# One list of timed steps for all five queues, single PSUM banks, and a reversing copy, in a Performer attention with an FNet block

## The chip, the cores and the metric

The kernel runs on one core of one Trainium2 chip. The core has TensorE (PE; its weight loads, which overlap, are PEld), VectorE (DVE), ScalarE (ACT), GpSimd (POOL) and SyncE (SP). Each takes its instructions in order from a queue of its own; DMAs are issued from SP, ACT or POOL and run on 16 DMA engines. The metric is the time of one execution on the device, in microseconds (us).

## The reference

All sizes: batch 8, heads 8, 576 rows, head dimension 64, 128 features; the MLP goes from 512 to 2048 and back. The MLP's weights come as float64.

```python
def phi(x):                          # for q and k, scaled
    proj = einsum('bhsd,md->bhsm', x, omega)
    h = proj - sum(x * x, -1) / 2
    return exp(h - max(h)) / sqrt(m)
kv = einsum('bhsm,bhsd->bhmd', k_p, v);  z = sum(k_p, axis=2)
attn = (q_p @ kv) / (q_p @ z + 1e-06)
x = attn with its heads side by side                 # (8, 576, 512)
u = x + real(fft(fft(x, axis=1), axis=2))
un = (u - mean(u)) / sqrt(var(u) + 1e-06)            # over the last axis
out = u + maximum(un @ w_ch1, 0) @ w_ch2
```

## The kernel before, in words

The work has four kinds of pieces, and each is written as a generator of steps (a stream).

- **Pairs** (`attn`): 32, each two heads of one batch, four per batch. k and q of the pair are loaded (`kq`, two buffers) and turned on TensorE in nine blocks (`transposed`: tps, evicted by ACT to kqT and later to qeT). Nine products with omega give 18 feature blocks (pp); DVE takes the maximum of each (nmx) and ACT the exponential (e). Nine products with v make kv (kvp, gathered in one PSUM bank), the q features are turned, and 36 matmul instructions give numerator and denominator (ndp), which DVE divides into xo. SP stores xo to DRAM (`xs`).
- **Mixing** (`mix`): one per batch, once the four pairs are stored. The Fourier transform along the rows uses symmetry: x needs rows 0 to 288 and the same rows reversed. The straight half is loaded by SP; the reversed half is gathered by three indirect DMAs from POOL with a table of row numbers (`turned`), 97 rows each. DVE folds sums, then POOL folds differences; TensorE multiplies with cosine and sine tables (yp, then ab), ACT and DVE combine, and DVE and POOL add to x. The result `us` goes to DRAM, one half by SP, the reversed half by three indirect scatters from POOL, 96 rows each.
- **Norm and MLP** (`prep`, `mlp`): 12 blocks of 384 rows. u is loaded, normalized by DVE with POOL's power, and turned (tp, unT). The first layer makes 16 tiles hp, whose Relu goes to ACT and DVE in turn, in two PSUM banks (mm); the second layer gathers 16 products in op, DVE adds u (`ur`), SP stores the output.
- **Weights** (`weights`, `narrow`): 32 tiles of 512 KB. POOL loads raw float64 words (three buffers) and clamps the high words; then ACT, DVE and POOL rebuild float32 from the bits, for which DVE runs four operations (lines 251, 255, 258, 259) and POOL the final sum (line 260).

PSUM is split into two double banks (`big`), two single ones (`sml`) and two for the MLP (`mm`).

`Listing.run` decides the order: it simulates the streams with the durations written into each `Step` and always takes the step that can start first. A `Step` has TensorE's time (`pe`), PSUM slots it holds and a chain of what follows on other engines. Only TensorE's queue keeps that order (`manual_schedule(engines={PE})`); the other four queues are ordered by the framework's own estimates. The gather is a chain entry of 9.0 us (line 425). From the 13th pair on each stream of pairs makes a pause of `PACE` = 25 us in the simulation (line 658). Of steps that can start at the same time the stream that stands first wins: norms, mixing, the two streams of pairs, weights, then the MLP (`channels`).

Of the kernel before, what the change touches and what calls it, by code (L numbers as in the profile page):

```python
# [29 lines left out]
ACT, DVE, POOL, DMA = "act", "dve", "pool", "dma"  # L30
HOP = 0.1


class Step:
# [4 lines left out]
    def __init__(self, pe=0.0, slots=(), chain=(), needed=True, when=None):  # L39
        self.pe, self.slots, self.chain = pe, slots, chain  # L40
        self.needed, self.when = needed, when


class Listing:
# [3 lines left out]
    def __init__(self, slots):  # L48
        self.free = {ACT: 0.0, DVE: 0.0, POOL: 0.0}
        self.slots = {name: [0.0] * n for name, n in slots.items()}  # L50
        self.now = 0.0

    def start(self, step, ready):
        if step.when is not None and not step.when():
            return None
        t = ready
        for name in step.slots:
            t = max(t, min(self.slots[name]))
        return t

    def run(self, streams):
        todo = [[g, next(g), 0.0] for g in streams]
        while todo:
            best = None
            for item in todo:
                t = self.start(item[1], item[2])
                if t is not None and (best is None or max(t, self.now) < best[0]):
                    best = (max(t, self.now), item)
            if best is None:
                raise RuntimeError("every stream waits")  # L70
            begin, item = best
            step = item[1]
            end = begin + step.pe
            if step.pe:
                self.now = end
            t = end
            for eng, dur in step.chain:
                t += HOP
                if eng in self.free:
                    t = self.free[eng] = max(t, self.free[eng]) + dur  # L80
                else:
                    t += dur
            for name in step.slots:
                at = self.slots[name]
                at[at.index(min(at))] = t
            item[2] = t + HOP if step.needed else end
            try:
                item[1] = next(item[0])
            except StopIteration:
                todo.remove(item)  # L90

HI_HIGH = float(np.uint32((1151 << 20) - 1).view(np.float32))
# [30 lines left out]
def kernel(  # L125
# [25 lines left out]
    CVB = 2  # L151
# [18 lines left out]
    cvt = ctx.enter_context(tc.tile_pool(name="cvt", bufs=CVB + 1))  # L170
    mlpp = ctx.enter_context(tc.tile_pool(name="mlp", bufs=2))
    dram = ctx.enter_context(tc.tile_pool(name="dram", bufs=1, space=bass.MemoryType.DRAM))
    big = ctx.enter_context(tc.tile_pool(name="big", bufs=2, space=PSUM))
    sml = ctx.enter_context(tc.tile_pool(name="sml", bufs=2, space=PSUM))
    mmp = ctx.enter_context(tc.tile_pool(name="mmp", bufs=2, space=PSUM))

    def big_tile(name):
        return big.tile([128, 2, 512], F32, name=name, tag="big")

    def sml_tile(name):  # L180
        return sml.tile([128, 512], F32, name=name, tag="sml")


    loaded = {}

    def load(n):
        b, pr = divmod(n, NP)
        h = slice(2 * pr, 2 * pr + 2)
        kq = ld.tile([P, 2 * R, D], F32, name="kq", tag="kq")
        rows = "i (p r) d -> (i p) r d"  # L190
        nc.sync.dma_start(kq[:, 0:R, :], k[b, h].rearrange(rows, r=R))
        nc.sync.dma_start(kq[:, R : 2 * R, :], q[b, h].rearrange(rows, r=R))
        loaded[n] = kq

# [7 lines left out]
    def load_v(n):  # L202
        b, pr = divmod(n, NP)
        vd = vds[n % NV]
        for i in range(2):
            nc.sync.dma_start(
                vd[D * i : D * i + D, :, (D + 1) * i : (D + 1) * i + D],
                v[b, 2 * pr + i].rearrange("(p r) d -> p r d", r=R),
            )
        loaded["v", n] = vd  # L210
# [4 lines left out]
    for n in range(NV):  # L215
        load(n)
        load_v(n)
# [4 lines left out]
    nc.gpsimd.memset(mhalf[:], -0.5)  # L222

    tabs = _tables(S, DM)
    tab_sb = {}
    for n, a in tabs.items():
        tab_sb[n] = const.tile(list(a.shape), F32, name=n + "_sb")
        src = nc.inline_tensor(a, name="k_" + n).ap()
        for p0, p1 in ((0, 96), (96, a.shape[0])):
            nc.scalar.dma_start(tab_sb[n][p0:p1], src[p0:p1])  # L230
    cs, sn, cd, sd = (tab_sb[n] for n in ("cs", "sn", "cd", "sd"))


    rows_hi = (S - CW * np.arange(NC3)[None, :] - np.arange(CP)[:, None]) % S
    turned = const.tile([CP, NC3], U32, name="turned")
    src = nc.inline_tensor(np.ascontiguousarray(rows_hi).astype(np.uint32), name="k_turned").ap()
    nc.scalar.dma_start(turned[:], src)
# [6 lines left out]
    def narrow(dst, raw):  # L244
# [18 lines left out]
    there = {"w1": 0, "w2": 0}  # L263

    def weights():
        parts = [
            (w1[:, j, f : f + CV], w1v[:, j, f : f + CV], "w1", f + CV if j == NDC - 1 else f)
            for f in range(0, DFF, CV)
            for j in range(NDC)
        ] + [(w2[:, j, :], w2v[:, j, :], "w2", j + 1) for j in range(NFC)]  # L270
        raws = []
        for i in range(len(parts) + CVB):
            if i < len(parts):
                dst, src = parts[i][:2]
                if src.dtype == F32:
                    nc.gpsimd.dma_start(dst, src)
                else:
                    raw = cvt.tile([128, CV, 2], U32, name="raw", tag="raw")
                    nc.gpsimd.dma_start(raw[:].rearrange("p n two -> p (n two)"), src.bitcast(U32))
                    raws.append(raw)  # L280
            if i >= CVB:
                dst, src, name, upto = parts[i - CVB]
                if src.dtype != F32:
                    yield Step(chain=((POOL, 0.8), (DVE, 2.8)))
                    narrow(dst, raws[i - CVB])
                there[name] = upto


    om2 = const.tile([128, 2, MF], F32, name="om2")
    nc.gpsimd.memset(om2[:], 0.0)  # L290
    omps = sml_tile("omps")
    nc.tensor.transpose(omps[:, 0:128], om[:].rearrange("m i d -> m (i d)"), ident[:])
    for i in range(2):
        rows = slice(D * i, D * i + D)
        nc.vector.tensor_scalar(om2[rows, i, :], omps[rows, 0:128], SCALE, None, op0=ALU.mult)


    xs = [dram.tile([S, DM], F32, name=f"xs{b}") for b in range(B)]
    us = [dram.tile([S, DM], F32, name=f"us{b}") for b in range(B)]

    def transposed(src, name):

        dst = att.tile([128, R, 128], F32, name=name, tag="turned")
        ps = big_tile("tps")
        p1 = sml_tile("tps1")
        for j in range(R):
            to = ps[:, j // 3, j % 3 * 128 :] if j < 6 else p1[:, (j - 6) * 128 :]
            nc.tensor.transpose(to[:, 0:128], src(j), ident[:])  # L310
        nc.scalar.activation(
            out=dst[:, 0:6, :].rearrange("q (two c) p -> q two (c p)", two=2),
            in_=ps[:, :, 0:384],
            func=AF.Copy,
        )
        nc.scalar.activation(
            out=dst[:, 6:9, :].rearrange("q c p -> q (c p)"), in_=p1[:, 0:384], func=AF.Copy
        )
        return dst

    done = {}

    def attn(n):
        b, pr = divmod(n, NP)
        yield Step(1.0, ("big", "sml"), ((ACT, 1.3),))
        kq, vd = loaded.pop(n), loaded.pop(("v", n))

        flat = kq[:].rearrange("p c d -> p (c d)")
        kqT = transposed(lambda j: flat[:, 128 * j : 128 * j + 128], "kqT")
        if n + NV < B * NP:  # L330
            load(n + NV)

# [35 lines left out]
        def feature(c):  # L368
            return es[c // 8][:, c % 8, :]
# [330 lines left out]
```

## Time and profile before

| | us |
|---|---|
| median of 3 runs (1616.69 to 1622.35) | 1617.15 |
| the profiled execution | 1618.99 |
| its span, from the first to the last instruction | 1617.2 |
| PE busy | 1449.6 (90%) |
| PEld busy | 905.3 (56%) |
| DVE busy | 456.9 (28%) |
| ACT busy | 339.3 (21%) |
| POOL busy | 324.8 (20%) |

Busy times are sums of instructions over the span. Matmuls are pipelined, so PE's busy time also holds the time in which a matmul runs at a lower clock; the granted clock (1.00 is full speed) stands beside it in the windows. Releasers of waits are inferred from semaphore events.

### The profile page before, as it was taken

The numbers are of one execution on the slowest core, as the hardware profiler recorded it, in microseconds if no ns is written. First come the engines' busy times: TensorE is split into PE (matmuls) and PEld (weight loads), VectorE is DVE, ScalarE is ACT, GpSimd is POOL, SyncE is SP. The second block draws the span as 40 slices with busy tenths as digits, with TensorE's granted clock in tenths as the row PEclk, the third lists the DMA queues.
The fourth block names the chain that finished last, engine by engine and source line by source line (L and its number), as shares of the span: only waits on it lengthen the run. The fifth ranks groups of instructions, "written<-read, shape, count | busy, mean of one in ns | idle before, by whom it ended". The sixth has DMA issues, their size and how long they took to land.

```text
span 1617.2 us, 15802 instructions
## 1 busy us (share of the span) xinstructions
PE 1449.6 (90%) x6241; PEld 905.3 (56%) x6241; DVE 456.9 (28%) x926; ACT 339.3 (21%) x925; POOL 324.8 (20%) x282
## 2 busy tenths in 40 slices
PE   5464647998999899899989989997999999999999
PEld 4453535764765576476656647555555454545453
DVE  3675763331312323132232323122110101010010
ACT  4443233231222123122212312121000000000000
POOL 5676852203102300310230031012100000000000
PEclk9776768998999999899989999998999999999999
DMA  6444433222223122222312221021110101010100
GB/s 182 139 138 110 133 121 97 63 82 65 72 59 101 47 59 70 65 72 54 102 46 65 69 66 50 15 70 32 46 38 5 53 0 59 0 59 0 40 0 26
DMA packets 132191, 103.98 MB, mean 64 GB/s; under 512 B 98596, under 2 KB 98852, under 8 KB 132118
## 3 DMA queue, kind: packets, MB, share of 16 engines
q1 hardware_dynamic: 106128, 75.63, 16.4%
q0 software_dynamic: 25344, 26.41, 5.8%
q8 instruction: 49, 0.80, 0.2%
q10 hardware_dynamic: 646, 0.94, 0.2%
q14 instruction: 24, 0.20, 0.0%
HBM read 74.50 MB, written 28.31 MB: 64 GB/s over the span
## 4 chain that ended last, share of the span: by engine, by line
PE 71%; DMA 12%; POOL 9%; DVE 4%; issue 3%; ACT 1%; SPq 0%; POOLq 0%; DVEq 0%; ACTq 0%
PE hp L601 30%; PE op L633 24%; DMA x<-xs,turned 7%; PE pp L345 4%; DMA raw<-in_moe_w_ch_dram 3%; PE kvp L374 3%; PE tps L310 3%; PE yp L471 3%; POOL raw L250 2%; POOL x L433 2%; PE ndp L394 2%; POOL w L260 1%; PE ab L488 1%; DMA xs<-xo 1%; DVE nmx L351 1%
## 5 line engine op out<-in xcount | busy, mean ns | idle before, releaser
L601 PE MATMUL hp<-unT,w 128*128 128x384 f32 x1536 | 514.5, 491 | 8.7 <-DVE ht L610 8.7
L633 PE MATMUL op<-w,ht 128*128 128x512 f32 x1152 | 506.8, 593 | 0.0
L601 PEld LDWEIGHTS hp<-unT,w 128*128 128x128 f32 x1536 | 291.5, 192 | 204.4 <-issue 10.7
L633 PEld LDWEIGHTS op<-w,ht 128*128 128x128 f32 x1152 | 215.4, 190 | 247.3 <-issue 243.9
L360 ACT ACTIVATE e<-pp,nmx 128x128 f32<-128x128 f32 x576 | 154.4, 405 | 182.0 <-DVE nmx L351 181.9
L345 PE MATMUL pp<-om,kqT 128*128 128x256 f32 x576 | 142.3, 399 | 18.2 <-ACT e L360 10.2
L610 DVE TENSOR_SCALAR ht<-hp 128x384 f32<-128x384 f32 x96 | 53.5, 557 | 356.8 <-PE hp L601 356.8
L612 ACT ACTIVATE ht<-hp 128x384 f32<-128x384 f32 x96 | 47.9, 499 | 492.8 <-PE hp L601 492.8
L565 POOL TENSOR_TENSOR rstd<-rstd,mhalf 128x1 f32<-128x1 f32 x36 | 20.9, 583 | 644.1 <-DVE rstd L564 635.7
L345 PEld LDWEIGHTS pp<-om,kqT 128*128 128x128 f32 x576 | 114.1, 202 | 43.7 <-ACT e L360 11.1
L351 DVE TENSOR_REDUCE nmx<-pp 128x8 f32<-128x1024 f32 (+1 forms) x96 | 89.6, 951 | 97.4 <-PE pp L345 97.0
L640 DVE TENSOR_TENSOR ur<-ur,op 128x512 f32<-128x512 f32 x36 | 24.6, 685 | 282.6 <-PE op L633 282.6
L374 PEld LDWEIGHTS kvp<-vd,e 128*128 128x128 f32 x576 | 76.9, 209 | 14.8 <-ACT e L360 7.6
L374 PE MATMUL kvp<-vd,e 128*128 128x130 f32 x576 | 78.2, 295 | 6.5 <-ACT e L360 6.5
L250 POOL TENSOR_SCALAR raw<-raw 128x512 f32<-128x512 f32 x32 | 67.7, 2117 | 49.2 <-DMA raw<-in_moe_w_ch_dram 49.0
L433 POOL DMA_INDIRECT x<-xs,turned x24 | 52.9, 2205 | 111.6 <-issue 67.5
L471 PE MATMUL yp<-cs_sb,fold 97*128 97x289 f32 x96 | 36.2, 540 | 34.5 <-DVE fold L457 31.3
L310 PE MATMUL tps<-ident,kq 128*128 128x128 f32 x288 | 43.7, 303 | 24.2 <-issue 11.2
L471 PE MATMUL yp<-sn_sb,fold 97*128 97x289 f32 x96 | 38.1, 568 | 24.4 <-ACT y L478 24.4
L310 PEld LDWEIGHTS tps<-ident,kq 128*128 128x128 f32 x288 | 37.5, 157 | 35.9 <-issue 18.3
L394 PE MATMUL ndp<-kv,qeT 128*64 128x65 f32 x1152 | 42.1, 230 | 15.4 <-DVE kv L382 14.0
L394 PEld LDWEIGHTS ndp<-kv,qeT 128*64 128x64 f32 x1152 | 37.9, 143 | 30.8 <-issue 28.7
(63 smaller groups left out, 901.2 us busy)
## 6 DMA issues: line engine op xcount, KB each, us to landing
raw<-in_moe_w_ch_dram POOLq DMA_DIRECT2D x32, 512.0 KB, 4.4
kq<-in_k_dram SPq DMA_DIRECT2D x32, 288.0 KB, 3.9
kq<-in_q_dram SPq DMA_DIRECT2D x32, 288.0 KB, 3.6
vd<-in_v_dram SPq DMA_DIRECT2D x64, 144.0 KB, 3.2
xs<-xo SPq DMA_DIRECT2D x64, 144.0 KB, 2.4
out_dram<-ur SPq DMA_DIRECT2D x36, 256.0 KB, 2.0
u<-us SPq DMA_DIRECT2D x32, 256.0 KB, 2.6
ur<-us SPq DMA_DIRECT2D x32, 256.0 KB, 2.6
```

Source lines behind the costliest of these rows:

```text
L250: nc.gpsimd.tensor_scalar(hif, hif, -HI_HIGH, HI_HIGH, op0=ALU.max, op1=ALU.min)
L310: nc.tensor.transpose(to[:, 0:128], src(j), ident[:])
L345: nc.tensor.matmul(flat_ps[:, 256 * j : 256 * j + 256], lhsT=kqT[:, 4 * t + j, :], rhs=om2[:].rearrange("p i m -> p (i m)"),)
L351: nc.vector.tensor_reduce(nmx[:], flat_ps[:, 0 : MF * num].rearrange("p (c m) -> p c m", m=MF), axis=AX.X, op=ALU.max, negate=True,)
L360: nc.scalar.activation(out=e[:, c, :], in_=flat_ps[:, MF * c : MF * c + MF], func=AF.Exp, bias=nmx[:, c : c + 1],)
L374: nc.tensor.matmul(kvp[:, 0 : 2 * (D + 1)], lhsT=feature(r), rhs=vd[:, r, :], start=(r == 0), stop=(r == R - 1),)
L394: nc.tensor.matmul(ndp[cols, r // 5, (D + 1) * (r % 5) : (D + 1) * (r % 5 + 1)], lhsT=qeT[:, r, cols], rhs=kv[:, i, :],)
L433: nc.gpsimd.indirect_dma_start(out=x[:, NC3 + c, :], out_offset=None, in_=rows[:, :], in_offset=bass.IndirectOffsetOnAxis(ap=turned[:, c : ...
L471: nc.tensor.matmul(yp[:, 0:NK], lhsT=fold[:, c, n, :], rhs=tab[:, c, :], start=(c == 0), stop=(c == NC3 - 1),)
L601: nc.tensor.matmul(hp[:], lhsT=w1[:, dc, 128 * fc : 128 * fc + 128], rhs=unT[:, dc, :], start=(dc == 0), stop=(dc == NDC - 1),)
L610: nc.vector.tensor_scalar(ht[:], hp[:], 0.0, None, op0=ALU.max)
L633: nc.tensor.matmul(yp[:], lhsT=hs[fc][:, 128 * i : 128 * i + 128], rhs=w2[:, fc, :], start=(fc == 0), stop=(fc == NFC - 1),)
```

## The change

What it does:

- A `Step` now belongs to one engine (PE, ACT, DVE, POOL, SP, or none), has a time there and a lateness after it (a DMA's landing, an eviction's end), names the events it waits for (`after`) and makes, and the buffers it takes and gives. A stream can `Fork`. `Listing` keeps all buffers and the five queues, and all five keep its order. Every DMA on SP is a step. A Relu goes to ACT or DVE, whichever ends first in the list.
- PSUM: six single banks for everything but the MLP's two. A pair's features come in groups of 4, 4, 4, 4, 2 instead of 8, 8, 2; the transposes are evicted in groups of 4, 4, 1 blocks instead of 6, 3.
- The reversed rows: after each pair's xs store, SP copies the pair's columns of rows 575 down to 288 into a second DRAM tensor `xb`; the mixing loads the reversed half from `xb` straight. The gather goes; the scatter of `us` stays.
- `narrow` has no clamp: high words beyond float32's range are no longer limited. ACT reads the raw high words and writes the scaled value to the destination first; DVE's four operations and POOL's sum follow.
- Tables are loaded by SP after the second pair's inputs instead of by ACT at the start; the weights start after the second pair's q has landed.

```diff
+    def __init__(self, eng, us=0.0, late=0.0, after=(), makes=None, take=(), give=()):
...
+    def start(self, step, ready, before):
+        t = ready[0] if before in step.engines and len(step.engines) == 1 else ready[1]
+        for ev in step.after:
+            if ev not in self.made:
+                return None
+            t = max(t, self.made[ev])
...
+        eng = min(step.engines, key=lambda e: max(t, self.free[e]) + step.engines[e])
+        return max(t, self.free[eng] if eng != NONE else 0.0), eng
...
+            end = begin + step.engines[eng]
+            self.free[eng] = end
+            done = end + step.late + (HOP if eng != NONE else 0.0)
...
+            item[3], item[4] = (end, done), eng
...
+    psum = ctx.enter_context(tc.tile_pool(name="psum", bufs=6, space=PSUM))
...
-        nc.gpsimd.tensor_scalar(hif, hif, -HI_HIGH, HI_HIGH, op0=ALU.max, op1=ALU.min)
-        nc.vector.tensor_scalar(bits, hi, 0x80000000, None, op0=ALU.bitwise_and)
-        nc.scalar.activation(out=hif, in_=hif, func=AF.Copy, scale=2.0**-112)
+        yield Step(ACT, 0.7, after=(("raw", i),))
+        nc.scalar.activation(out=dst, in_=hif, func=AF.Copy, scale=2.0**-112)
+        yield Step(DVE, 0.6)
+        nc.vector.tensor_scalar(hi, hi, 0x80000000, None, op0=ALU.bitwise_and)
+        yield Step(DVE, 1.15)
         nc.vector.scalar_tensor_tensor(
-            bits, hi, 3, bits, op0=ALU.logical_shift_left, op1=ALU.bitwise_or
+            bits, bits, 3, hi, op0=ALU.logical_shift_left, op1=ALU.bitwise_or
         )
         nc.vector.tensor_scalar(hi, bits, 0xFF800000, None, op0=ALU.bitwise_and)
+        yield Step(DVE, 0.7)
         nc.vector.scalar_tensor_tensor(lof, lo, 2.0**-52, hif, op0=ALU.mult, op1=ALU.mult)
+        yield Step(POOL, 1.3, makes=("w", i), give=("raw",))
         nc.gpsimd.tensor_tensor(out=dst, in0=dst, in1=lof, op=ALU.add)
...
-        for t, num in enumerate((8, 8, 2)):
+        for t, num in enumerate((4, 4, 4, 4, 2)):
...
+        yield Step(SP, 1.2, 2.6, give=("xo",))
         for i in range(2):
             h = 2 * pr + i
             nc.sync.dma_start(
                 xs[b].rearrange("(p r) c -> p r c", r=R)[:, :, h * D : (h + 1) * D],
                 xo[D * i : D * i + D],
             )
-        done["attn", b] = done.get(("attn", b), 0) + 1
+
+        yield Step(SP, 0.6, 3.0, makes=("x", b, pr))
+        cols = slice(2 * pr * D, (2 * pr + 2) * D)
+        nc.sync.dma_start(
+            xb[b][:, cols].rearrange("t (i d) -> i t d", i=2),
+            xs[b][S - 1 : S // 2 - 1 : -1, cols].rearrange("t (i d) -> i t d", i=2),
+        )
...
-        yield Step(chain=((DMA, 9.0),), when=lambda: done.get(("attn", b), 0) == NP)
+        yield Step(SP, 1.6, 4.6, after=tuple(("x", b, pr) for pr in range(NP)), take=("x",))
         x = fft.tile([CP, NR, DM], F32, name="x", tag="x")
...
-        for c in range(NC3):
-            nc.gpsimd.indirect_dma_start(
-                out=x[:, NC3 + c, :],
-                out_offset=None,
-                in_=rows[:, :],
-                in_offset=bass.IndirectOffsetOnAxis(ap=turned[:, c : c + 1], axis=0),
-            )
+        nc.sync.dma_start(
+            hi[1:CP], xb[b].rearrange("(c p) d -> p c d", p=CW)
+        )
+        nc.sync.dma_start(hi[0:1, 0, :], xs[b][0:1, :])
+        nc.sync.dma_start(hi[0:1, 1:NC3, :], xb[b][CW - 1 : 2 * CW : CW, :].unsqueeze(0))
...
+        yield from folds(0, DVE, (1.8, 1.0, 0.56), take=("half",))
+        yield Fork(folds(1, POOL, (3.5, 1.85, 1.1), take=("half",)))
...
         for n in range(start, B * NP, 2):
             if n >= 3 * NP:
-                yield Step(chain=((DMA, PACE),))
+                yield Step(NONE, late=PACE)
             yield from attn(n)
...
-    with tc.manual_schedule(engines={mybir.EngineType.PE}):
+    with tc.manual_schedule(
+        engines={every.PE, every.DVE, every.Activation, every.Pool, every.SP}
+    ):
...
-            [norms(), mixing(), pairs(0), pairs(1), weights(), channels()]
+            [first(), loads(), norms(), mixing(), pairs(0), pairs(1), channels(), weights()]
```

`attn` begins with another step on no engine, `Step(NONE, after=(("kq", n), "om2"))`. The second layer's steps are now two products long (1.72 us) instead of four; a first layer's step stays at 2.6 us.

## Rows read from the trace of the kernel before

**Rows 1.** Windows of four stretches: length, busy time (instructions) by engine, granted clock, DMA share.
```profile
0.00:229.00 229.00, 123.38 (x761) 103.25 (x761) 142.64 (x231) 81.60 (x218) 152.56 (x128) 0.76 0.51 145
229.00:400.00 171.00, 151.39 (x818) 103.50 (x819) 57.98 (x129) 51.41 (x150) 43.53 (x33) 0.93 0.27 73
400.00:1195.00 795.00, 756.33 (x3494) 480.85 (x3493) 209.29 (x475) 179.91 (x506) 123.74 (x114) 0.97 0.21 60
1195.00:1617.20 422.20, 418.47 (x1170) 217.67 (x1168) 47.00 (x92) 26.33 (x52) 4.93 (x9) 1.00 0.08 25
```

**Rows 2.** Chain that ended last: start us, us, what; pieces at clock 1.00.
```profile
433.42 3.88 PE pp L345 x18
...
1117.40 5.86 PE yp L471 x24
...
1195.82 41.28 PE hp L601 x128
...
1279.61 41.28 PE hp L601 x128
```

**Rows 3.** Timeline of the steady stretch, PE: start us, us, engine, line, operation.
```profile
638.05 2.18 PE L374 MATMUL kvp<-vd,e 128*128 128x130 f32 x18
...
644.58 1.27 PE L394 MATMUL ndp<-kv,qeT 128*64 128x65 f32 x36
...
652.75 1.15 PE L310 MATMUL tps<-ident,kq 128*128 128x128 f32 x9
...
691.25 0.60 PE L488 MATMUL ab<-cd_sb,y 128*97 128x129 f32 x4
...
692.59 0.66 PE L488 MATMUL ab<-cd_sb,y 128*97 128x129 f32 x4
```

**Rows 4.** Lines of the first 230 us, POOL and DVE: busy us, mean ns; idle before.
```profile
L250 POOL TENSOR_SCALAR raw<-raw 128x512 f32<-128x512 f32 x32 | 67.7, 2117 | 49.2 <-DMA raw<-in_moe_w_ch_dram 49.0
...
L251 DVE TENSOR_SCALAR w<-raw 128x512 uint32<-128x512 uint32 x31 | 29.6, 954 | 46.4 <-POOL raw L250 46.4
L255 DVE SCALAR_TENSOR_TENSOR w<-raw,w 128x512 uint32<-128x512 uint32 x30 | 28.9, 965 | 5.3 <-ACT raw L254 5.1
L258 DVE TENSOR_SCALAR raw<-w 128x512 uint32<-128x512 uint32 x30 | 22.5, 754 | 0.1
...
L259 DVE SCALAR_TENSOR_TENSOR raw<-raw 128x512 f32<-128x512 uint32 x30 | 21.6, 724 | 0.2
```

**Rows 5.** One line's instructions (258): ns min/median/max, first and last start.
```profile
L258 DVE TENSOR_SCALAR raw<-w x32: 389/420/3556, 25.8 to 236.6; 128x512 uint32<-128x512 uint32 x32
```

**Rows 6.** Timeline of the start, SP's queue.
```profile
117.28 2.77 SPq L416 DMA_DIRECT2D xs<-xo  x3
...
205.74 1.29 SPq L555 DMA_DIRECT2D u<-us  x3
```

**Rows 7.** Line 601 in the first 260 us: ns min/median/max, first and last start.
```profile
L601 PE MATMUL hp<-unT,w x32: 486/486/847, 234.1 to 259.8; 128*128 128x384 f32 x32
```

**Rows 8.** Timeline of the steady stretch, SP's queue and DVE.
```profile
647.26 1.24 SPq L416 DMA_DIRECT2D xs<-xo  x2
...
670.19 1.76 DVE L448 TENSOR_TENSOR half<-x 97x1536 f32<-97x1536 f32 x1 [9.80 <-DMA x<-xs,turned]
```

**Rows 9.** Tile x, 640 to 700 us, the scatter shown: first and last start.
```profile
L525 POOL DMA_INDIRECT us<-x,turned x1: 967/967/967, 698.6 to 698.6; - x1
```

**Rows 10.** DMA issues: queue, count, KB each, median us to landing.
```profile
xs<-xo SPq DMA_DIRECT2D x64, 144.0 KB, 2.4
...
x<-xs SPq DMA_DIRECT2D x8, 576.0 KB, 4.6
...
x<-xs,turned POOLq DMA_INDIRECT x24, 13.7
us<-x,turned POOLq DMA_INDIRECT x24, 2.9
```

**Rows 11.** Waits of PE over the whole span: total us, times, longest.
```profile
PE tp L573 <- DVE rstd L564: 18.0, 1, 18.0
```

More of the change, by code (lines that the diff above doesn't have):

```diff
@@ L27 @@
 CP = CW + 1
-ACT, DVE, POOL, DMA = "act", "dve", "pool", "dma"
-HOP = 0.1
+PE, ACT, DVE, POOL, SP, NONE = "pe", "act", "dve", "pool", "sp", "none"
+HOP = 0.15
 class Step:
-    def __init__(self, pe=0.0, slots=(), chain=(), needed=True, when=None):
-        self.pe, self.slots, self.chain = pe, slots, chain
-        self.needed, self.when = needed, when
-class Listing:
[L48 to L59, printed above, removed]
-    def run(self, streams):
-        todo = [[g, next(g), 0.0] for g in streams]
+    def __init__(self, eng, us=0.0, late=0.0, after=(), makes=None, take=(), give=()):
+        self.engines = eng if isinstance(eng, dict) else {eng: us}
+        self.late, self.after, self.makes = late, after, makes
+        self.take, self.give, self.eng = take, give, None
@@ L319, in transposed, with softmax @@
-        return dst
-    done = {}
+    def softmax(n, t, num, ps, es):
+        yield Step(DVE, 0.15 + 0.135 * num)
+        nmx = small.tile([P, 4], F32, name="nmx", tag="nmx", bufs=4)
+        nc.vector.tensor_reduce(
+            nmx[:, 0:num],
+            ps[:, 0 : MF * num].rearrange("p (c m) -> p c m", m=MF),
+            axis=AX.X,
+            op=ALU.max,
+            negate=True,
+        )
+        yield Step(
+            ACT, 0.255 * num, 0.12, take=("e" if num == 4 else "e1",), give=("bank",), makes=("e", n, t)
+        )
+        e = att.tile([P, num, MF], F32, name="e", tag=f"e{num}", bufs=8 if num == 4 else 2)
+        for c in range(num):
+            nc.scalar.activation(
+                out=e[:, c, :],
+                in_=ps[:, MF * c : MF * c + MF],
+                func=AF.Exp,
+                bias=nmx[:, c : c + 1],
+            )
+        es[t] = e
@@ L381, in attn @@
-        kv = att.tile([128, 2, D + 1], F32, name="kv", tag="kv")
-        nc.vector.tensor_copy(
-            out=kv[:].rearrange("m i d -> m (i d)"), in_=kvp[:, 0 : 2 * (D + 1)]
-        )
-        if n + NV < B * NP:
-            load_v(n + NV)
-        yield Step(1.0, ("big", "sml"), ((ACT, 1.3),))
-        qeT = transposed(lambda r: feature(R + r), "qeT")
-        yield Step(1.4, ("big",), ((DVE, 1.5), (DMA, 3.0)))
-        ndp = big_tile("ndp")
+            yield Fork(softmax(n, t, num, ps, es))
@@ new lines, in attn, with keep @@
+        kvs = []
+        def keep():
+            yield Step(DVE, 0.3, take=("kv",), give=("bank",), makes=("kv", n))
+            kv = att.tile([128, 2, D + 1], F32, name="kv", tag="kv")
+            nc.vector.tensor_copy(
+                out=kv[:].rearrange("m i d -> m (i d)"), in_=kvp[:, 0 : 2 * (D + 1)]
+            )
+            kvs.append(kv)
+        yield Fork(keep())
+        qeT = yield from transposed(
+            lambda r: feature(R + r),
+            "qeT",
+            lambda j0, j1: tuple(("e", n, t) for t in range((R + j0) // 4, (R + j1 - 1) // 4 + 1)),
+            ("qeT", n),
+            lambda j0, j1: {4: ("e",), 8: ("e",), R: ("e1",)}[j1],
+        )
@@ L586, with hidden @@
     outf = out.rearrange("b s d -> (b s) d")
     def mlp(j):
-        hs = []
+        hs = {}
+        def hidden(fc, hp):
+            step = Step(
+                {ACT: 0.15 + TB / 1130.0, DVE: 0.15 + TB / 945.0},
+                late=0.1,
+                take=("ht",),
+                give=("mm",),
+                makes=("ht", j, fc),
+            )
+            yield step
+            ht = mlpp.tile([128, TB], F32, name="ht", tag="ht", bufs=NFC)
+            if step.eng == DVE:
+                nc.vector.tensor_scalar(ht[:], hp[:], 0.0, None, op0=ALU.max)
+            else:
+                nc.scalar.activation(out=ht[:], in_=hp[:], func=AF.Relu)
+            hs[fc] = ht
@@ L590, in mlp @@
         for fc in range(NFC):
             yield Step(
+                PE,
                 8 * TB / 1193.0,
-                ("mm",),
-                ((DVE if fc % 2 else ACT, 0.6),),
-                needed=False,
-                when=lambda: done.get("prep", 0) > j and there["w1"] >= 128 * fc + 128,
+                after=tuple(("unT", j, i) for i in range(NTT))
+                + tuple(("w", fc * 128 // CV * NDC + dc) for dc in range(NDC)),
+                take=("mm",),
+                give=("unT",) if fc == NFC - 1 else (),
```

580 lines of the change are left out of this document (316 added, 264 removed).

## The prediction

> **What bounds the kernel now.** I read the windows of the whole span first, in four stretches: up to the first matmul of the MLP, the time until the last weights are in use, the stretch in which attention, mixing and MLP run mixed, and the pure MLP at the end [rows 1]. The reader is to see two columns, TensorE's busy time and its granted clock. At the end TensorE is busy for 418 of 422 us at clock 1.00. In the first 229 us it is busy for 123 us at a mean clock of 0.76.
>
> Next, what TensorE's work takes at clock 1.00, from the chain of waits and the timeline [rows 2, 3]. One MLP block of 384 rows, from one first layer to the next, is 1279.61 - 1195.82 = 83.8 us; there are 12, 1005.5 us. A head pair is two sets of nine transposes (1.15 each), pp 3.88, kvp 2.18 and ndp 1.27, 9.6 us, and 32 pairs are 308 us. A mixing is yp 5.86 and three ab blocks that start 692.59 - 691.25 = 1.34 apart, 9.9 us, and 8 are 79 us. Together that is 1393 us. The span is 1617.2, so 224 us are lost. The windows say where: busy time times clock is 94, 141, 734 and 418 us of full-speed work, so the stretches lose some 135, 30, 61 and 4 us (230; the two ways agree within 6).
>
> Then the lines of the first 230 us [rows 4], to see who holds the start. The clamp on POOL takes 67.7 us there, and DVE stood still for 46.4 us waiting for it. The four DVE operations of the weights' narrowing take 29.6 + 28.9 + 22.5 + 21.6 = 102.6 of DVE's 142.6 us; so the pairs and the mixing, some 40 us, are the smaller part. An operation that takes 0.39 us at its fastest took 3.56 at its slowest [rows 5]. The timeline shows the result: the fourth pair's rows leave at 117 us [rows 6] and the first hp starts at 234.1 [rows 7].
>
> Last, the steady stretch [rows 8]: from a batch's last xs store (647.26) to the first fold (670.19) go 22.9 us, of which the gather's landing is the largest part (13.7) [rows 10]. The old list counted 9.0 us for it, so PE, which keeps the list's order, stands before yp once per batch.
>
> **The change part by part.**
>
> *Narrowing without the clamp.* POOL loses 67.7 us and DVE the 46.4 us wait [rows 4]; ACT starts from the landed tile. The four DVE operations stay: now 3.4 us a tile (their four means), at least 2.2 if the two single-input ones ran at their fastest, near 0.4, and the other two at 0.7. With less POOL work beside them I take 2.6. Over 30 tiles that is 78 us in place of 103.
>
> *The gather replaced by a copy.* Per batch three POOL issues go and two steps come on SP: the reversed copy xb after each pair's xs, and a straight load of x. xs lands in 2.4 us for 144 KB in 256-byte pieces; xb moves twice that in the same pieces, from DRAM to DRAM, which no row shows. Bounds: 2.4 (as one xs) and 13.7 (as the gather). I take 4, nearer xs, whose pieces it shares. With issues, xs to fold is then 1.2 + 2.4 + 0.6 + 4 + 1.6 + 4.6 = 14.4 us against 22.9 [rows 8, 10]. The new list counts about 13.8 (its own figures: 1.2 + 2.6 + 0.6 + 3.0 + 1.6 + 4.6 and hops), so the wait left on PE is small: I take 2 to 4 us for a batch, in place of the present 61 us over six of them.
>
> Behind x's load on SP stand the next kq, u and ur loads and the out stores; behind the fold on DVE stand the pairs' maxima and every Relu that the list gave to DVE. If x is late, those wait, and PE with them as soon as its two mm banks are full.
>
> *Single banks and smaller steps.* A pair now has five maxima and six evictions instead of three and four: each extra instruction repeats a fixed part of a few tenths of a us, under 1 us a pair on DVE and on ACT. The cover is large: in 400 to 1195 DVE is busy for 209 of 795 us and ACT for 180 [rows 1]. Without that cover, 32 pairs would cost at most some 30 us. In exchange a softmax can start after four features. I count this at nothing either way.
>
> *One list for five queues.* Every queue keeps the list's order, also where a duration in it is wrong. A late item costs what it is late beyond the slack of PE's next steps (1.7 to 2.6 us each). The pause of 25 us before later pairs no longer acts: it is a step on no engine, and the step behind it, on no engine either, takes the end without the lateness. So attention runs as early as it can, ahead of the MLP. TensorE's work is the same and the MLP fills what is left, but more waits fall close together. At nothing this costs 0; if one in two pairs holds PE for 2 us, 32 us. I take 10.
>
> **The sum.** First hp: DVE sets the pace of four pairs, with 12 weight tiles beside them: 10 us until inputs are there, 4 x 5 for the pairs (the 40 us above over seven pairs and a mixing, with the extra maxima), 12 x 2.6 for the tiles, and about 7 for the tail of the fourth: 68 us. Then 14.4 to the fold. From fold to the last us in the steady stretch: 698.6 - 670.2 + 2.9 = 31 us [rows 8 to 10]. From the u load to the first hp it is now 234.1 - 205.7 = 28 us [rows 6, 7], of which PE waited 18.0 for the DVE and POOL queues [rows 11]: 10. That makes 124; with a tenth for misses of the list, 135. By then about 8 pairs and one mixing are done, 87 us at full speed: a loss of 48 in place of 135. After it I leave 20 of the present 30 us, since w2's tiles still have to come; 7 batches at 3 us are 20, and 10 for the denser list: 30 in place of 61. The end stays at 3. Span: 1393 + 48 + 20 + 30 + 3 = 1494. The profiled execution took 1618.99, 1.8 above its span and also 1.8 above the median of the runs, 1617.15, so the span's number serves for the time: **1493 us**.
>
> **The rivals.**
>
> *The copy runs on few DMA engines.* Two indirect transfers in this kernel differ by one row: the gather of 97 rows lands in 13.7 us, the scatter of 96 rows in 2.9 [rows 10]. So how a transfer's outer size divides decides its time here, and xb's outer size is two (`i t d`, i = 2). Spread over two engines, each has 288 pieces: by bytes 13.7 x 74/199 = 5 us, by pieces 13.7 x 288/97 = 41 us, and I take 12. Then x is 9 us later than the list counts at each batch; less 2 to 3 of slack, over seven or eight batches, this gives back some 45 us: 1538. Against it: xs, in the same pieces, is quick. The Trainium skill states the rule (DMA: Bandwidth & Descriptors, section on why a DMA increments its semaphore by 16): a transfer runs on the largest number of engines up to 16 that divides the slowest dimension of both sides, which is 1 for 97, 16 for 96 and 2 here. By that rule the trace's 13.7 and 2.9 agree, and xb is slow.
>
> *The start stays with DVE.* If the four operations keep 3.4 us a tile and the fixed order puts weights ahead of pairs, the four pairs are done near 100 us and the first hp starts near 185: a loss of 95, and 1540 to 1590. For it: DVE's share now [rows 4]. Against it: the wait of 46.4 us had its cause in the clamp.
>
> *The lists hold each other, and it is slower.* At the start, landings vary: if a queue stands for a late DMA, all five stand. The place is the 32 pairs, each with some 45 steps on five queues. To be slower, the new list has to lose 224 us on PE, for instance 2 us at the start of 10 steps of each batch and 60 us more before the first hp: 1640. Before, three of the queues could be ordered around such a miss by their own estimates. Against it: the stretch 400 to 1195 keeps PE to a fixed order too and loses only 61 us in it.
>
> **How the numbers follow.** Forecast 0.52, few engines 0.28, start with DVE 0.11, lists 0.09. The forecast alone spans 1450 to 1535: 2.4 against 8 us for xb is 25 us, 110 against 150 us for the first hp is 25 us. For 8 in 10 I take 1445 to 1565, which holds the second case and half of the third. Faster by over 0.5% (8 us, about what a measurement here can tell): 0.90; within: 0.02; slower: 0.08.
>
> **What the profile after would show.** Right: first hp between 115 and 150 us, POOL's busy time down by the clamp's 67.7 us and more, first stretch's clock above 0.76, xb landing in 3 to 6 us, PE's waits before yp under 4 us each, and the last pair done before 700 us. Wrong: xb landing at 10 us or more with SP waiting before the x load (second case); DVE busy at 9 tenths until 180 us (third); PE idle in most slices before 500 us with short waits on many releasers (fourth).

## The result, and the profile after

The changed kernel takes 1488.97 us (median of 4 runs, 1488.18 to 1492.52) against 1616.92 for the kernel before on the same chip: a ratio of 0.9206, with a 95% interval of 0.9181 to 0.9231. The forecast was 1493.

The profiled execution of the changed kernel has a span of 1486.8 us. First its windows, the first four with the borders of [rows 1], the last up to its own first hp; columns as there.

```profile
0.00:229.00 229.00, 175.84 (x1214) 145.04 (x1214) 149.50 (x301) 109.45 (x321) 83.61 (x94) 0.88 0.59 161
229.00:400.00 171.00, 159.46 (x1064) 120.01 (x1063) 79.41 (x188) 76.89 (x240) 45.40 (x47) 0.97 0.45 122
400.00:1195.00 795.00, 789.53 (x3173) 471.79 (x3172) 152.86 (x373) 171.16 (x463) 73.51 (x81) 1.00 0.19 54
1195.00:1486.80 291.80, 288.15 (x794) 147.43 (x792) 17.11 (x36) 28.30 (x57) 3.80 (x6) 1.00 0.08 27
...
0.00:153.00 153.00, 109.75 (x843) 95.45 (x844) 97.02 (x204) 78.86 (x239) 53.66 (x66) 0.85 0.63 169
```

As in the prediction, a stretch loses its length less PE's busy time times the clock. Before, the four stretches lost 135, 30, 61 and 4 us; now they lose 74, 16, 6 and 4 (229 - 175.84 x 0.88 = 74, and so on). So the 130 us came half from the start (61) and half from behind it (14 + 55). The clock is printed to two places, so the loss of the 795 us stretch is known to about 4 us where PE's clock is below 1.00, and that of the others to about 1.

Then the lines of the first layer, and of the narrowing on DVE in the first 300 us (columns of rows 7 and rows 4).

```profile
L724 PE MATMUL hp<-unT,w x1536: 483/486/590, 153.0 to 1441.5; 128*128 128x384 f32 x192
```

```profile
L279 DVE SCALAR_TENSOR_TENSOR w<-w,raw 128x512 uint32<-128x512 uint32 x32 | 27.3, 853 | 0.3
L284 DVE SCALAR_TENSOR_TENSOR raw<-raw 128x512 f32<-128x512 uint32 x32 | 24.9, 791 | 0.3
L282 DVE TENSOR_SCALAR raw<-w 128x512 uint32<-128x512 uint32 x32 | 19.6, 613 | 1.1
L277 DVE TENSOR_SCALAR raw<-raw 128x512 uint32<-128x512 uint32 x32 | 17.5, 564 | 12.8 <-ACT w L275 12.7
```

The first hp starts at 153.0 instead of 234.1 [rows 7]. The four operations take 89.3 us for 32 tiles, 2.8 a tile against 3.4 [rows 4]; DVE's 46.4 us wait for the clamp is a 12.7 us wait for ACT.

What still waits in the first 300 us, all engines, and the landings of the weights' loads (issued on line 300):

```profile
POOL w L286 <- DVE raw L284: 82.5, 23, 9.9
...
ACT w L275 <- DMA raw<-in_moe_w_ch_dram: 37.0, 10, 10.9
DVE half L515 <- DMA x<-xb: 29.2, 3, 12.9
```

```profile
DMA to landing us min/median/max: 3.7/5.1/10.3
```

The list counts 4.5 us for a weight's landing. Where one takes up to 10.3, ACT stands at the head of its fixed queue, for 37.0 us in all. DVE stands 29.2 us for the first three batches' reversed rows. SP's queue in the timeline shows why:

```profile
80.97 0.62 SPq L488 DMA_DIRECT2D xb<-xs  x1
81.71 3.31 SPq L220 DMA_DIRECT2D kq<-in_k_dram  x1
...
87.29 0.34 SPq L502 DMA_DIRECT2D x<-xb  x1
...
531.15 0.62 SPq L488 DMA_DIRECT2D xb<-xs  x1
531.88 4.22 SPq L226 DMA_DIRECT2D vd<-in_v_dram  x2
```

The load of x from xb, which waits for the last copy, goes 6.3 us after that copy was issued (5.9 to 6.4 over the eight batches); the list counts 0.6 + 3.0. A load right behind a copy holds SP, here for 3.3 and 4.2 us.

### The profile page after: what moved, and what is told of

Its sections match the earlier page's. It is cut to its first block, busy times and chain, and to the rows that moved or that the text cites. A ratio compares the mean times of both kernels' runs of the same rounds, so it can differ in the third digit from the quotient of the medians.

```text
span 1486.8 us, 16157 instructions
## 1 busy us (share of the span) xinstructions
PE 1413.0 (95%) x6241; PEld 884.3 (59%) x6241; DVE 398.9 (27%) x898; ACT 385.8 (26%) x1081; POOL 206.3 (14%) x226
## 4 chain that ended last, share of the span: by engine, by line
PE 80%; DMA 11%; DVE 3%; POOL 2%; issue 2%; ACT 1%; SPq 1%; DVEq 0%; POOLq 0%; ACTq 0%
PE hp L724 31%; PE op L747 31%; PE pp L398 5%; PE kvp L420 3%; DMA x<-xb 3%; DMA xb<-xs 2%; PE tps L337 2%; PE yp L555 2%; DMA raw<-in_moe_w_ch_dram 2%; PE ndp L457 1%; DMA xs<-xo 1%; PE ab L581 1%; PE tp L681 1%; DVE half L515 1%; ACT e L366 1%
## 5 line engine op out<-in xcount | busy, mean ns | idle before, releaser
L724 PE MATMUL hp<-unT,w 128*128 128x384 f32 x1536 | 502.9, 486 | 0.0
L710 ACT ACTIVATE ht<-hp 128x384 f32<-128x384 f32 x188 | 92.5, 492 | 683.4 <-PE hp L724 683.4
L354 DVE TENSOR_REDUCE nmx<-pp 128x4 f32<-128x512 f32 (+1 forms) x160 | 95.9, 631 | 65.8 <-PE pp L398 54.4
L420 PE MATMUL kvp<-vd,e 128*128 128x130 f32 x576 | 82.0, 300 | 7.8 <-ACT e L366 6.9
L515 POOL TENSOR_TENSOR half<-x 97x1536 f32<-97x1536 f32 x8 | 28.5, 3565 | 207.3 <-DVE rden L468 138.7
L286 POOL TENSOR_TENSOR w<-w,raw 128x512 f32<-128x512 f32 x32 | 44.0, 1380 | 95.3 <-DVE raw L284 82.5
L343 ACT ACTIVATE kqT<-tps 128x512 f32<-128x512 f32 (+1 forms) x96 | 42.5, 510 | 42.5 <-PE tps L337 42.2
L343 ACT ACTIVATE qeT<-tps 128x512 f32<-128x512 f32 (+1 forms) x96 | 41.1, 512 | 33.5 <-PE tps L337 33.5
L457 PEld LDWEIGHTS ndp<-kv,qeT 128*64 128x64 f32 x1152 | 36.9, 140 | 19.4 <-issue 17.7
L685 ACT ACTIVATE unT<-tp 128x512 f32<-128x512 f32 x36 | 19.5, 601 | 99.8 <-PE tp L681 99.8
L604 DVE SCALAR_TENSOR_TENSOR bmp<-ab,bmp 97x65 f32<-97x65 f32 x96 | 25.0, 326 | 71.2 <-ACT bmp L599 70.2
## 6 DMA issues: line engine op xcount, KB each, us to landing
vd<-in_v_dram SPq DMA_DIRECT2D x64, 144.0 KB
xs<-xo SPq DMA_DIRECT2D x64, 144.0 KB
```

Of the source, the lines that this page charges most:

```text
L343: nc.scalar.activation(out=dst[:, j0:j1, :].rearrange("q c p -> q (c p)"), in_=ps[:, 0 : 128 * (j1 - j0)], func=AF.Copy,)
L354: nc.vector.tensor_reduce(nmx[:, 0:num], ps[:, 0 : MF * num].rearrange("p (c m) -> p c m", m=MF), axis=AX.X, op=ALU.max, negate=True,)
L420: nc.tensor.matmul(kvp[:, 0 : 2 * (D + 1)], lhsT=feature(r), rhs=vds[n % NV][:, r, :], start=(r == 0), stop=(r == R - 1),)
L457: nc.tensor.matmul(ndp[r // 5][cols, (D + 1) * (r % 5) : (D + 1) * (r % 5 + 1)], lhsT=qeT[:, r, cols], rhs=kvs[0][:, i, :],)
L515: eng.tensor_tensor(out=h[:], in0=lo, in1=hi, op=op)
L710: nc.scalar.activation(out=ht[:], in_=hp[:], func=AF.Relu)
```

## The experiments

Each time is a median of four executions, with the kernel before timed beside them. That kernel's own medians differ by up to 5 us, so a difference between two rows of the table is known to some 5 us; the ratios are against the kernel before beside the same run. Except in the first and the last experiment, high words are not limited, as in the changed kernel. The table gives the loss of PE's full-speed time in the first three stretches of [rows 1], worked out from each kernel's windows as above; the last stretch loses 4 in all.

| kernel | us | 0 to 229 | 229 to 400 | 400 to 1195 |
|---|---|---|---|---|
| before | 1616.9 to 1622.1 | 135 | 30 | 61 |
| after | 1488.97 | 74 | 16 | 6 |
| 1 after, clamp back | 1492.45 | 72 | 17 | 8 |
| 2 after, gather of 97 rows back | 1504.59 | 82 | 25 | 9 |
| 3 after, list for PE alone | 1574.48 | 139 | 22 | 39 |
| 4 before, new narrowing | 1571.13 | 106 | 23 | 59 |
| 5 after, landings as measured | 1476.99 | 60 | 20 | 4 |
| 6 after, one copy a batch, 8 outermost | 1442.25 | 48 | 0 | 0 |
| 7 after, pause acts | 1490.27 | 78 | 20 | 6 |
| 8 after, SP not listed | 1505.45 | 75 | 17 | 23 |
| 9 after, one copy a batch, 2 outermost | 1485.24 | 66 | 15 | 16 |
| 10 as 6, landings as measured | 1431.56 | 39 | 2 | 1 |
| 11 after, gather of 96 rows | 1452.74 | 61 | 1 | 0 |
| 12 before, gather of 96 rows | 1532.41 | 135 | 1 | 0 |

**1. The clamp back in the new list**, and with it, which the expectation does not name, an empty step ahead of each of the two folds, which takes the fold's buffer.

```diff
-        yield Step(ACT, 0.7, after=(("raw", i),))
+        yield Step(POOL, 2.1, after=(("raw", i),))
+        nc.gpsimd.tensor_scalar(hif, hif, -HI_HIGH, HI_HIGH, op0=ALU.max, op1=ALU.min)
+        yield Step(ACT, 0.7)
```

> The changed kernel with the clamp put back as a listed POOL step of 2.1 us ahead of ACT's part; nothing else moves. If the clamp's removal carries a large part of the shorter start (theory A), POOL again has 67 us more in the first 300 us, the weights fall behind and the first hp moves from 153 to 170 us or later: 1510 to 1530 us. If the common list carries the gain (theory B), POOL has room (46 of the first 131 us busy) and the time stays within 1489 to 1500.

Measured: 1492.45 us, ratio 0.9217 (0.9192 to 0.9243), not to be told from the change itself: theory B. POOL is busy for 272.7 us in place of 206.3, and the first hp starts at 156.3. With POOL's queue in the list, the clamp's work fits in. The empty step was not run by itself.

**2. The three gathers back**, counted with the 2.5 us issue and 13.0 landing that rows show, on POOL's list; the copy goes.

```diff
-        nc.sync.dma_start(
-            hi[1:CP], xb[b].rearrange("(c p) d -> p c d", p=CW)
-        )
...
+        for c in range(NC3):
+            yield Step(POOL, 2.5, 13.0 if c == NC3 - 1 else 0.0, after=("turned",))
+            nc.gpsimd.indirect_dma_start(
+                out=x[:, NC3 + c, :],
...
```

> The changed kernel with the three indirect gathers on POOL back in place of the copy xb and the load from it, counted in the list with what they take (2.5 us each on POOL, landing 13 us after the last). Theory A: a batch's chain is some 8 us longer, which shows in full ahead of the first hp and in part later: 1500 to 1512. Theory B: a list that knows the landing fills it with MLP; only the first batch pays: 1489 to 1500.

Measured: 1504.59, ratio 0.9288 (0.9263 to 0.9314). Theory A's range holds. The copy is worth 15.6 us here (13 by the ratios), of the 91 us that the old kernel lost behind the start.

**3. Only PE's queue kept to the list.**

```diff
-        engines={every.PE, every.DVE, every.Activation, every.Pool, every.SP}
+        engines={every.PE}
```

> The changed kernel with only TensorE's queue kept to the list; DVE, ACT, POOL and SP ordered by the framework as before. Theory A: most of the gain stays: 1495 to 1530. Theory B: most of the gain goes: 1570 to 1650.

Measured: 1574.48, ratio 0.9717 (0.9692 to 0.9741). Two thirds of the gain are lost, and the start loses 139 us although nothing is clamped. PE's longest waits in the first 229 us, and ACT's timeline in that time:

```profile
PE pp L398 <- ACT kqT L343: 69.8, 2, 69.6
```

```profile
62.28 0.77 ACT L275 ACTIVATE w<-raw 128x512 f32<-128x512 f32 x1
66.55 0.67 ACT L275 ACTIVATE w<-raw 128x512 f32<-128x512 f32 x1 [3.49 <-DMA raw<-in_moe_w_ch_dram]
...
129.59 0.67 ACT L275 ACTIVATE w<-raw 128x512 f32<-128x512 f32 x1 [2.67 <-DMA raw<-in_moe_w_ch_dram]
```

The framework's estimates put the weight tiles one behind the other on ACT, which the new narrowing uses first. Each waits some 2.7 us for its load, and PE stands for 69.6 us, once, for an eviction queued behind them. That is theory B.

**4. The kernel before with the new narrowing**, its weights' step counted as (ACT 0.7, DVE 2.8).

```diff
-        nc.gpsimd.tensor_scalar(hif, hif, -HI_HIGH, HI_HIGH, op0=ALU.max, op1=ALU.min)
-        nc.vector.tensor_scalar(bits, hi, 0x80000000, None, op0=ALU.bitwise_and)
-        nc.scalar.activation(out=hif, in_=hif, func=AF.Copy, scale=2.0**-112)
...
+        nc.scalar.activation(out=dst, in_=hif, func=AF.Copy, scale=2.0**-112)
+        nc.vector.tensor_scalar(hi, hi, 0x80000000, None, op0=ALU.bitwise_and)
...
```

> The kernel before with the narrowing of the changed one (no clamp, large values not limited) and nothing else; its list counts 0.7 us of ACT and 2.8 us of DVE for a tile. Theory A: the first stretch's loss of 135 us shrinks by 40 to 70: 1545 to 1580. Theory B: under 20 us: 1597 or more.

Measured: 1571.13, ratio 0.969 (0.9662 to 0.9717). In the old kernel the clamp was worth 49 us, 29 of them at the start (135 to 106): theory A's time, with less at the start than the 40 to 70 that it named. So experiments 1 and 4 price the same edit at nothing in the new kernel and at 49 us in the old one. That the order of the queues makes this difference is argued; the two kernels differ in more, and the clamp was not put into experiment 3.

**5. Landings counted as the trace of after has them**: raw 8.0 for 4.5, xb 6.2 for 3.0, x 6.5 for 4.6, and the empty step of experiment 1.

```diff
-                yield Step(POOL, 0.6, 4.5, take=("raw",), makes=("raw", i))
+                yield Step(POOL, 0.6, 8.0, take=("raw",), makes=("raw", i))
...
-            yield Step(which, dur[0], **more)
+            yield Step(NONE, **more)
+            yield Step(which, dur[0])
```

> The changed kernel; only three landings counted in the list are changed: raw 8.0 us in place of 4.5 (measured median 5.1, up to 10.3), xb 6.2 in place of 3.0, x 6.5 in place of 4.6. If the loss left in the first 300 us (some 85 us) comes from queues that stand for a landing the list counted too early (theory C), ACT's 37 us and DVE's 61 us of such waits shrink and the time falls to 1465 to 1480. If it is the work of DVE and the DMAs themselves (theory D), it stays within 8 us of 1489, or a few us slower.

Measured: 1476.99, ratio 0.9136 (0.9107 to 0.9166): 12 us better, most of it at the start (74 to 60). ACT's 37.0 us wait for raw in the first 300 us is 1.5; DVE's 29.2 us for the reversed rows only falls to 20.1. The time is in theory C's range, and ACT's wait went as it had it; the empty step is not separated from the counts.

**6. One copy a batch with the 8 heads outermost**, in the same 256-byte pieces, in place of four with 2 outermost.

```diff
-            xb[b][:, cols].rearrange("t (i d) -> i t d", i=2),
-            xs[b][S - 1 : S // 2 - 1 : -1, cols].rearrange("t (i d) -> i t d", i=2),
+            xb[b].rearrange("t (h d) -> h t d", h=H),
+            xs[b][S - 1 : S // 2 - 1 : -1, :].rearrange("t (h d) -> h t d", h=H),
```

> The changed kernel with one copy xb a batch, heads outermost (8 in place of 2), 2304 pieces of 256 bytes in place of 576 four times, counted as 6.3 us after the last pair's xs. If the outer size sets the number of DMA engines (few engines), eight of them take 288 pieces each as two do now, and the one copy lands in about the same 6 us as the quarter of it does: 1480 to 1495. If a copy is spread over all engines anyway, four times the pieces take 15 us or more until the load of x can start: 1500 to 1515.

Measured: 1442.25, ratio 0.8917 (0.8895 to 0.894). SP's timeline, then the windows:

```profile
77.00 0.75 SPq L491 DMA_DIRECT2D xb<-xs  x1
...
83.58 0.34 SPq L501 DMA_DIRECT2D x<-xb  x1
```

```profile
229.00:400.00 171.00, 171.00 (x1199) 131.28 (x1197) 88.14 (x195) 82.47 (x262) 42.47 (x39) 1.00 0.47 125
400.00:1195.00 795.00, 795.00 (x2930) 458.23 (x2930) 139.73 (x341) 145.80 (x378) 67.50 (x78) 1.00 0.17 49
```

Four times the pieces take 6.6 us in this first batch (6.6 to 9.8 over the eight), as a quarter of them took 6.3: the side of the few engines, though the time lies 38 us below its range. PE shows no gap from 229 to 1195. Over the whole span DVE's folds wait 1.5 us for x from xb, against 60.9 in the change. How the 47 us divide between fewer copies that hold SP, folds that no longer wait, and the landing counted as 6.3 is not separated; experiment 5, which counts it as 6.2 with four copies, gains 12.

**9. One copy a batch with 2 outermost**, pieces of 1 KB: as few issues as in experiment 6, and the spread of the change.

```diff
-            xb[b].rearrange("t (h d) -> h t d", h=H),
+            xb[b].rearrange("t (h d) -> h t d", h=2),
```

> As e6 (one copy a batch, 1442 us), but with two halves of the columns outermost in place of eight heads: 576 pieces of 1 KB. If the outer size sets the engines, two engines move 295 KB each and the load of x starts 12 us or more after the copy in place of 6.6: 1450 to 1470. If e6 gains by issuing 8 copies in place of 32 and the spread is nothing, it is as e6: 1438 to 1447, or faster for a quarter of the pieces.

Measured: 1485.24, ratio 0.9168 (0.9145 to 0.9191); slower than either side expected, though the load starts more than 12 us after the copy, as the few engines' side had it. SP's timeline:

```profile
76.22 0.70 SPq L491 DMA_DIRECT2D xb<-xs  x1
76.97 10.01 SPq L498 DMA_DIRECT2D x<-xs  x1
...
92.27 0.34 SPq L501 DMA_DIRECT2D x<-xb  x1
```

The copy takes 14.6 to 18.1 us over the eight batches for the bytes that experiment 6 moved in 6.6 to 9.8, and DVE again waits 56.2 us for x from xb. So the number of issues does not set the time. The pieces are larger here as well, but the share of the 16 DMA engines that is busy points to the outer dimension. First in a stretch of this run, then in one of the change, in which a copy moves with nothing else beside it but one fetch of instructions (columns of rows 1):

```profile
609.50:617.00 7.50, 7.50 (x19) 3.40 (x18) 0.00 (x0) 0.00 (x0) 0.00 (x0) 1.00 0.14 48
...
648.00:650.50 2.50, 2.50 (x10) 1.44 (x9) 0.00 (x0) 0.49 (x1) 0.00 (x0) 1.00 0.15 35
```

0.14 and 0.15 of 16 engines are 2.2 and 2.4, for pieces of either size. The Trainium skill's rule (DMA: Bandwidth & Descriptors, section on why a DMA increments its semaphore by 16) gives 2 engines for these copies and 8 for experiment 6's. These runs agree with it.

**7. The pause of 25 us acts again.**

```diff
-                yield Step(NONE, late=PACE)
+                yield Step(NONE, PACE)
```

> The changed kernel with the pause of 25 us made to act (as time of a step in place of its lateness), from the 13th pair on. If the denser attention costs nothing (as counted in the forecast: 10 us), the time stays within 10 us of 1489; if the crowding of pairs costs waits, the paced list is faster by more than 10.

Measured: 1490.27, ratio 0.9204 (0.9184 to 0.9225). The last xs then goes at 831 us instead of 643, and the time stays: packing attention densely costs nothing that these runs can tell.

**8. SP left to the framework**, the other four queues listed.

```diff
-        engines={every.PE, every.DVE, every.Activation, every.Pool, every.SP}
+        engines={every.PE, every.DVE, every.Activation, every.Pool}
```

> The changed kernel with SP's queue left to the framework and the other four kept to the list. If the order of DMAs is what made the four queues' list worth 85 us, most of it goes: 1540 or more. If it is the order on DVE, ACT and POOL, it stays: 1485 to 1510.

Measured: 1505.45, ratio 0.9299 (0.9276 to 0.9322). SP's place in the list is worth 16 us, by the windows all in the steady stretch (23 against 6). Of the 86 us of experiment 3, 69 belong to DVE, ACT and POOL, and 64 of them lie in the first 229 us. That window, in experiment 3 and here:

```profile
0.00:229.00 229.00, 120.43 (x869) 103.18 (x869) 145.49 (x265) 92.56 (x260) 82.26 (x95) 0.75 0.53 150
...
0.00:229.00 229.00, 173.12 (x1213) 143.39 (x1214) 149.47 (x301) 108.67 (x321) 83.26 (x94) 0.89 0.62 165
```

**10. Experiment 6 with the landings as measured**: raw 8.0, the copy 0.7 and 5.0, x 4.6 and 6.0, and the empty step.

```diff
-        yield Step(SP, 0.6, 6.3, after=tuple(("x", b, pr) for pr in range(NP)), makes=("xb", b))
+        yield Step(SP, 0.7, 5.0, after=tuple(("x", b, pr) for pr in range(NP)), makes=("xb", b))
...
-        yield Step(SP, 1.6, 4.6, after=(("xb", b),), take=("x",))
+        yield Step(SP, 4.6, 6.0, after=(("xb", b),), take=("x",))
```

> As e6, with the landings counted in the list as measured there: raw 8.0 us in place of 4.5, and after the copy 5.0 and 4.6 us of SP and 6.0 until x is there. If what is left of the start's loss is missed landings (theory C), 1425 to 1435; if it is work (theory D), 1440 to 1450.

Measured: 1431.56, ratio 0.8827 (0.8802 to 0.8853), the fastest version: 57 us below the change, and within theory C's range. What is left is the start, 39 us.

**11. Experiment 2 with 96 rows in each gather**, the last one's landing counted as 4.0; SP loads the three rows that are left.

```diff
-                out=x[:, NC3 + c, :],
+                out=x[0:CW, NC3 + c, :],
...
-                in_offset=bass.IndirectOffsetOnAxis(ap=turned[:, c : c + 1], axis=0),
+                in_offset=bass.IndirectOffsetOnAxis(ap=turned[0:CW, c : c + 1], axis=0),
```

> As e2 (gathers in place of the copy, 1505 us), but each gather takes 96 rows in place of 97 and SP loads the three last rows; counted with 4.0 us to landing in place of 13.0. If 97 rows are slow because 97 does not divide over the engines, the gathers land in about 3 us like the scatters and the time falls to 1440 to 1465. If gathers are slow as such, they stay at 13 and the list, which now counts too little, makes it 1505 or slower.

Measured: 1452.74, ratio 0.896 (0.8943 to 0.8976): one row less, with the list's count set to suit, is worth 52 us. The gathers' landings and POOL's time for the issue, in experiment 2 and here:

```profile
x<-xs,turned_sb POOLq DMA_INDIRECT x24, 13.8
...
L496 POOL DMA_INDIRECT x<-xs,turned_sb x24: 2147/2167/2282, 82.4 to 657.2; - x24
```

```profile
x<-xs,turned_sb POOLq DMA_INDIRECT x24, 4.6
...
L499 POOL DMA_INDIRECT x<-xs,turned_sb x24: 916/927/1204, 84.0 to 573.2; - x24
```

**12. The kernel before with 96 rows in each gather**, the three rows loaded by SP, nothing else touched: old list, old queues, clamp.

```diff
+            nc.sync.dma_start(x[CW:CP, NC3 + c, :], rows[r : r + 1, :])
...
-                out=x[:, NC3 + c, :],
+                out=x[0:CW, NC3 + c, :],
```

> The kernel before with its list, its clamp and its queues as they were; only each gather moves 96 rows in place of 97, and SP loads the three rows left over. It tells whether the old kernel's waits before yp came from the gather's landing. Theory D (PE stood before yp because the gather landed 4.7 us later than the 9.0 that the list counts): the gather lands in about 4.6 us as in the last experiment, the 31.3 us in which PE waited before yp for DVE's fold all but go, and the time is 1585 to 1595. Rival E (the fold's place among DVE's other work holds it, and the clamp holds the start, so an earlier landing is only waited for elsewhere): PE's waits before yp for the fold stay above 20 us and the time is 1605 to 1620.

Measured: 1532.41, ratio 0.9463 (0.944 to 0.9485). Both sides expected too small a gain. Its windows:

```profile
0.00:229.00 229.00, 119.95 (x770) 99.06 (x771) 138.04 (x243) 87.63 (x237) 155.16 (x130) 0.78 0.49 145
229.00:400.00 171.00, 170.29 (x977) 117.69 (x977) 63.26 (x150) 50.13 (x141) 40.75 (x41) 1.00 0.31 86
400.00:1195.00 795.00, 795.00 (x3574) 495.54 (x3573) 210.13 (x466) 180.62 (x507) 99.46 (x106) 1.00 0.21 61
```

The start is untouched (135), and of the 91 us behind it 1 is left. The three old gathers of one batch in the trace of the kernel before (view and stretch of rows 9):

```profile
L433 POOL DMA_INDIRECT x<-xs,turned x3: 2149/2179/2257, 651.7 to 656.7; - x3
```

The last issue starts 5.0 us after the first and lands some 13.7 after its own start, so the fold starts 18.5 us behind the first issue (651.7 to 670.19 [rows 8]), where the list counts 9.0. In all eight batches DVE stands for this landing, 17.7 to 19.7 us behind the first issue. The seven batches behind 229 us are late by 66 us in all. With 96 rows the last issue starts 2.5 us after the first and 4.6 more make 7.1, early against the list. What makes up the other 24 us (the clock, POOL's shorter issues, the order that the framework makes anew) is not separated.

The expectation had counted PE's waits before yp for the fold alone, 31.3 us. 16.1 of them lie in the start, where 14.6 stay. Behind 229 us PE waited 36.1 us before yp in the kernel before, for the fold, for ACT's y and for e, and waits 0.7 now. The stretch 400 to 1195 lost 38.7 us in idle time and 756.33 x 0.03 = 23 in busy time at clock 0.97 [rows 1]; here, without the gaps, its clock is 1.00.

## Why the prediction came out, step by step

**The floor of 1393 us** held: 1486.8 - 1393 = 94, against 74 + 16 + 6 + 4 = 100 by the windows, the same 6 apart as before the change; the shortest span, experiment 10's, is 1432.1.

**The total was right because misses cancelled.** Behind a first hp forecast at 135 us the losses were to be 48, 20, 30 and 3. By 153.0, where hp did start, the loss is 153 - 109.75 x 0.85 = 60 us: 12 more. By 400 us it is 90 against 68 forecast; from 400 to 1195 it is 6 against 30. So 22 us too few and 24 too many made a total that is 4 us off, which is luck.

**The start: its cause wrong.** The first hp came at 153.0, 18 us after the forecast and just outside its 115 to 150. The working gave the gain to the clamp: POOL's 67.7 us and DVE's 46.4. The 2.6 us a tile was near (2.8), and POOL's busy time fell by more than the clamp (324.8 to 206.3). But with the lists the clamp costs nothing (1). In the old kernel its removal takes a fifth of the start's loss away (4), and with the new streams in the framework's order the start loses 139 us without any clamp (3). What carries it is the order on DVE, ACT and POOL: the start loses 75 us with it and 139 without (8 against 3). The working priced that order at no gain, only at a risk. The step that failed is "One list for five queues": it asked what a fixed order costs and not what the framework's order was costing; no row in the prediction shows that order.

**xb was mis-sized, between forecast and rival.** Taken at 4 us, it lands in some 6; the rival took 12. The working gave the copy twice the bytes of an xs store; the trace lists 144.0 KB for either. The rival's mechanism fits (6, 9, 11), and its price for one copy was too high: with 2 outermost, 288 pieces in each take 6 us, near its bound by bytes of 5. The forecast's two to four us a batch then came out smaller in the steady stretch, but three batches in the first 300 us paid 29.2 us on DVE. And the copy's whole cost was larger than either term: one copy a batch with 8 outermost takes 47 us off the change (6), 26 of them at the start, near the 45 that the rival would have added. Against that kernel the forecast, which held no such cost, would have been some 50 us too high (1493 against 1442).

**The steady stretch was explained right, and what would remain of it was put too high** (30 us, measured 6): 61 us were lost for the gather being late against the list. Experiment 12 shows it, within the rounding of the clock, and that the 30 us of the stretch 229 to 400 had the same cause, which the forecast had left to w2's tiles. The working spread the 61 us over six batches; the trace has five gathers in that stretch and two in the one before it. But experiment 2 shows that shortening the transfer was not needed for most of it: with the same slow gather counted as 13.0, the new list loses 25 + 9 us there. That it has other work for PE meanwhile is the likely reason, not shown.

**The 10 us for the denser list** are not there (7). The third case, the start staying with DVE at 3.4 us a tile, did not come; nor did the fourth: late landings did hold the lists, but counting them as measured returned 12 us (5). The last pair was to be done before 700 us: its xs goes at 643. PE's waits in the first 153 us are led by these, none before yp:

```profile
PE pp L398 <- DVE xo L472: 11.4, 1, 11.4
PE pp L398 <- ACT kqT L343: 10.4, 2, 7.6
PE tp L681 <- DVE u L677: 7.3, 1, 7.3
```

**Open.** No run separates the single PSUM banks and the smaller groups. A copy with rows outermost, which could spread further, was not tried. What the remaining 39 us at the start of experiment 10 would need was not taken apart, nor was experiment 12's edit tried together with experiment 4's.

## What to carry to other kernels

Where queues keep a written order, read for each transfer its landing against what the list counts, and multiply the lateness by how often it comes: 9.5 us x 7 was most of this kernel's loss behind its start, and one row less in a gather returned nearly all of it. Then price an edit under the order that will hold: the clamp was worth 49 us in the kernel whose queues the framework ordered and nothing in the one with the list. A total that comes out right proves none of its terms.

## What the runs showed of the hardware

- A gather of 97 rows lands in 13.7 us and takes POOL 2.18 us to issue; of 96 rows, 4.6 and 0.93.
- Copies from DRAM to DRAM, from the issue to the load that waits for them: 576 pieces of 256 bytes with 2 outermost 5.9 to 6.4 us in the change, 2304 with 8 outermost 6.3 to 9.8 (experiments 6 and 10), 576 pieces of 1 KB with 2 outermost 14.6 to 18.1. With 2 outermost 0.14 to 0.15 of the 16 DMA engines are busy meanwhile.
- Behind such a copy the next DMA mostly holds SP's queue: 3.3 and 4.2 us in the two places shown from the change, 3.7 to 6.9 in experiment 6 and 8.3 to 11.8 in experiment 9, where the issue of the load of x from xs took 0.33 to 0.34 in the kernel before. That this is the copy's backlog is inferred from the place alone.
